# Four one-bank PSUM tiles for one four-bank tile, one store per output tile, and a new table of ranks, in a fused attention and two-layer kernel

## The chip, the cores and the metric

The kernel runs on one core of a Trainium2 chip. The metric is the device time in microseconds of one execution. Five engines work side by side: PE multiplies matrices into PSUM (eight banks of 512 floats in each of 128 partitions), DVE, ACT and POOL do elementwise work, and SP issues the transfers. Each engine takes its own instructions strictly in the order in which they were written for it, and an instruction that waits for a semaphore holds up all behind it on its engine.

## The reference, cut to what matters

Batch 2, 8 heads, 768 positions, head size 64, six hash bits; then two layers of 1536 tokens by 512 by 2048.

```
mask = q_bucket[:, :, :, None] == k_bucket[:, :, None, :]      # six sign bits of q @ proj, k @ proj
scores = np.where(mask, scale * np.matmul(q, k.transpose(0, 1, 3, 2)), -1e9)
attn = np.exp(scores - np.max(scores, axis=-1, keepdims=True))
attn = attn / (np.sum(attn, axis=-1, keepdims=True) + 1e-09)
x = np.matmul(attn, v)                       # then heads side by side: (1536, 512)
h = x @ w_in                                 # first layer
g = P(h) / (Q(h) + 1e-06)                    # cubic over quadratic in |h|
x = g @ w_out
h = x @ w_in2                                # second layer
g = h * np.clip(h + 3.0, 0.0, 6.0) / 6.0
return g @ w_out2
```

## The kernel before, in words

All values that go through PE are split into a high and a low part, and each product is three matmuls (high by high, high by low, low by high). The weights arrive as 64-bit floats in tiles of 512 KB and are converted on the chip by ACT, DVE and POOL.

**Attention** has 48 groups: 16 heads, each with three groups of 2 x 128 query rows. The names in the plan are: S, four matmuls that make the scores of 128 rows (L369 and L372) in one of two score buffers of two banks each; M, their maximum on DVE (L376); E, the exponential on ACT; A and N, the normalising; P, four transposes on PE (L403) that put a quarter of a 512-wide tile each into one bank; H, the copy of that bank to SBUF, on ACT or DVE (L413); V, the 24 matmuls with the values (L419); VO, their copies. Two groups in six do not go through P, H and V: DVE transposes them, and W (b_mm, L457) multiplies them with small 32-row tiles into all four banks, which OC and VA (b_out) then empty. TP (L244) transposes the queries and keys of a head, TF copies them out on ACT ("tf"), Z and ZB ("bt", L281 and L287) make the hash bits. SPH, SPL and SB (L268, L274, L294) are transfers on SP's queue that spread a head's parts over the operands of S; LQ and LV load queries, keys and values (L162, L172, L174).

**The layers** are 96 steps: two layers of three blocks of 512 tokens, each with 16 steps. A step has 12 matmuls into "h" (L509), the elementwise function, and 12 matmuls (L577) that add into four banks, one for each 128 outputs, over the 16 steps of a block. At the end of a block f0 and f1 empty the four banks: in layer one as a high part on ACT and a low part on DVE (L584), in layer two as a copy (L592 or ACT) that goes to the output.

**PSUM**: four of the eight banks hold the scores, and later h. The other four are handed out in turn by bank(): P, TP, Z, V and the tables at the start all take the next one. In the layers the same four are the sums of L577.

**Order**: nothing is left to a scheduler on the chip. ordered() simulates the five engines with the durations in W and picks, whenever an engine is free, the ready piece of work with the least rank; ranks are b = g * W_SLOT plus OFF and SIX. The pieces are then written in that order. Semaphore waits are put in where two instructions touch the same tile.

Of the kernel before, what the change touches and what calls it, by code (L numbers as in the profile page):

```python
# [5 lines left out]
F32 = mybir.dt.float32  # L6
# [3 lines left out]
ALU = mybir.AluOpType  # L10
# [3 lines left out]
B, H, S, D = 2, 8, 768, 64  # L14
# [12 lines left out]
NPRE = 12  # L27
NMID = 5
WARM = 8
CVS = (-4, 1, 8, 9, 11, 19, 26, 26, 36, 39, 43, 44)  # L30
RING = {"raw": 3, "cvd": 3, "t1": 2, "t2": 3, "t3": 2, "t4": 1, "gh": 2, "gl": 2}

W = {"S": 0.70, "M": 0.87, "E": 0.89, "A": 0.42, "N": 0.97, "N_A": 0.74, "B": 0.87, "W": 1.40, "P": 0.44, "H": 0.485, "H_D": 0.60, "V": 2.72, "VO": 0.35, "OC": 0.47, "VA": 0.62,
# [5 lines left out]
W_LAG = {"PE": 0.25, "DVE": 0.13, "ACT": 0.16, "POOL": 0.09, "SP": 2.5, "NONE": 0.0}  # L39
LAG = {"A": 0.30, "E": 0.26, "ld": 3.0, "LQ": 2.8}  # L40
LOOK = [0.486, 0.308]
ZERO = (0.0,) * 6
SIX = {"S": [-3.13, -2.02, -6.82, -6.23, -1.8, -1.85], "M": [24.01, 16.96, -9.66, -7.6, -7.88, -19.37], "E": [-3.33, 26.26, -14.76, 8.01, 16.22, 8.9],
# [3 lines left out]
LIKE = {("N", "ACT"): 0, ("H", "DVE"): 0.3, ("TL", "POOL"): 0, ("TH", "ACT"): 0.3, ("lo", "POOL"): 2, ("hi", "ACT"): 2}  # L47
W_SLOT = 5.7086

OFF = {"B": -4.172, "W": 17.16, "S": -18.746, "rr": -0.257, "M": 14.723, "E": -32.07, "A": 4.967, "N": -0.925, "P": 13.629, "H": 3.752, "V": -8.005,  # L50
       "VO": -33.348, "XH": 18.534, "XL": 4.581, "TP": 16.446, "Z": 11.887, "c": -5.304, "SPH": -3.253, "SPL": -22.357, "SB": -20.361, "LQ": -29.686, "LV":
       -24.74, "ld": -25.955, "cf": 5.747}
AHEAD = 0.9324
FILL = {("TP", 1, 1): 3, ("S", 1, 1): 6}
RINGS = {"T": 4, "S": 2, "p": 6, "pt": 8}

# [1 line left out]
def body(tc, q, k, v, proj, moe_w_in, moe_w_out, moe_a, moe_b, moe2_w_in, moe2_w_out, out):  # L58
    nc = tc.nc

    def act(out, in_, func=ACTF.Copy, **kw):
        nc.scalar.activation(out=out, in_=in_, func=func, **kw)  # L62
# [17 lines left out]
    atl = tc.alloc_tile_pool(name="atl", bufs=1, side="right")  # L80
    ate = tc.alloc_tile_pool(name="ate", bufs=1)
    psum = tc.alloc_tile_pool(name="psum", bufs=1, space=bass.MemoryType.PSUM)
    banks = psum.tile([128, 4, 512], F32, name="banks")
    used_banks = [0]

    def bank(n):
        used_banks[0] += 1
        return banks[:, (used_banks[0] - 1) % 4, 0:n]

    psc = tc.alloc_tile_pool(name="psc", bufs=1, space=bass.MemoryType.PSUM)  # L90

# [63 lines left out]
    nat, tf, hl, lr, live = {}, {}, {}, {}, {}  # L155
# [57 lines left out]
    for i, p in enumerate((f(pjh), pjl)):  # L213
        for isk in range(2):
            rows = slice(64 * isk, 64 * isk + 64)
            nc.vector.tensor_tensor(out=zl[rows, i, 128 + 32 * isk:128 + 32 * isk + 2 * NB].rearrange("p (a b) -> p a b", a=2),
                                    in0=p[rows].unsqueeze(1).to_broadcast([64, 2, NB]), in1=sgn[rows], op=ALU.mult)
# [135 lines left out]
    sps, ptile, pts, xts = {}, {}, {}, {}  # L353
# [91 lines left out]
    def b_mm(g, part):  # L445

        vs, pb = nat[("v", g // 3)], pts[("b", g // 3)]
        if part == 0:
            for _ in range(4):
                bank(0)  # L450
        for j in range(R * part, R * part + R):
            for i in range(4):
                rows = slice(32 * i, 32 * i + 32)
                for c in range(2):
                    x = j + NK // 2 * c
                    at = (R * (x % 4) + x // 4 - R * i) % NK
                    nc.tensor.matmul(out=banks[64 * c:64 * c + 64, i, 0:128], lhsT=vs[rows, at], rhs=pb[rows, :, 32 * x:32 * x + 32],  # L457
                                     start=(j == 0), stop=(j == NK // 2 - 1))
        if part:
            pts.pop(("b", g // 3))  # L460

    def b_out(g, part):
        main, rest = slice(64, 128), slice(0, 64)
        if part == 0:
            live["ot"] = atl.tile([128, 4, 128], F32, name="ot", tag="ot")
            act(live["ot"][main], banks[rest, :, 0:128])
            return
        nc.vector.tensor_tensor(out=xts[1][main].rearrange("p (x i k) -> p i x k", x=4, i=4),
                                in0=banks[main, :, 0:128].rearrange("p i (x k) -> p i x k", x=4),
                                in1=live["ot"][main].rearrange("p i (x k) -> p i x k", x=4), op=ALU.add)  # L470

    def x_part(g):
        hd, rg = divmod(g, 3)
# [15 lines left out]
    mps, acc = {}, {}  # L489
# [96 lines left out]
    def fin_o(m, i):  # L586
        b, r = divmod(4 * steps[m][1] + i, R)
        last = steps[m][1] == NBLK - 1
        tag = ("t3", "t2", "t1", "t3")[i] if last else "t3"
        o = mps["mp"].tile([128, 512], F32, name="o2", tag=tag, bufs=RING[tag])  # L590
        if (i % 2 == 1) != last:
            nc.vector.tensor_copy(out=o, in_=acc["o"][i])  # L592
        else:
            act(o, acc["o"][i])
        dst = out[b * S:(b + 1) * S].rearrange("(k a r) d -> r a k d", a=4, r=R)[r]
        for a in range(4):
            nc.sync.dma_start(out=dst[a], in_=o[32 * a:32 * a + 32])


    work = {}  # L600
# [7 lines left out]
    def plan_attention():  # L608
        T = W_SLOT
        pool = ("POOL",)  # L610

        def pair(pr):
# [3 lines left out]
            for hd in heads:  # L616
                if hd > 2:
                    add(("LQ", hd), ("SP", W["LQ"]), (g0 - 9 + 2 * (hd % 2)) * T + OFF["LQ"], [("TP", hd - 2, 1)], lambda e, hd=hd: load_qk(hd))
                for n in range(2):
                    r = (g0 - 9 + 2 * (hd % 2) + n) * T + OFF["TP"]  # L620

                    old = [("Z", pr - 1), ("TL", hd - 2)]
                    add(("TP", hd, n), ("PE", W["TP"]), r, [("LQ", hd)] + old, lambda e, hd=hd, n=n: tp_mm(hd, n), takes=("T",),
                        earliest=2.0 if pr == 1 else 0.0)
                    add(("TF", hd, n), ("ACT", W["TF"]), r + 0.6, [("TP", hd, n)], lambda e, hd=hd, n=n: tp_full(hd, n), frees=(("TP", hd, n),))
                add(("TH", hd), {"ACT": W["TH"], "POOL": W["TH_P"]}, r + 1.2, [("TF", hd, 0), ("TF", hd, 1), ("SPH", hd - 1), ("SPL", hd - 1)],
                    lambda e, hd=hd: tp_hi(hd, e), pool)
                add(("TL", hd), {"DVE": W["TL"], "POOL": W["TL_P"]}, r + 1.8, [("TH", hd)], lambda e, hd=hd: tp_lo(hd, e), ("POOL", "DVE"))
                r = (g0 - 4 + 3 * (hd % 2)) * T
                old = [("S", 3 * (hd - 2) + 2, 1)]  # L630
                add(("SPH", hd), ("SP", W["SPH"]), r + OFF["SPH"], [("TH", hd)] + old, lambda e, hd=hd: spread_hi(hd))
                add(("SPL", hd), ("SP", W["SPL"]), r + OFF["SPL"], [("TL", hd), ("SPH", hd)], lambda e, hd=hd: spread_lo(hd))
            r = (g0 - 5) * T + OFF["Z"]
            which = (0, 1) if pr else (1,)
# [3 lines left out]
            for hd in heads:  # L638
                r = (g0 - 4 + 3 * (hd % 2)) * T
                add(("SB", hd), ("SP", W["SB"]), r + OFF["SB"], [("ZB", pr), ("SPH", hd)], lambda e, hd=hd: spread_bits(hd))  # L640

# [4 lines left out]
        def group(g):  # L646
# [4 lines left out]
            def at(x):  # L651
                return b + OFF[x] + SIX.get(x, ZERO)[g % 6]

# [65 lines left out]
    def release_l():  # L719
        atl.release()  # L720
        wpool[2] = tc.alloc_tile_pool(name="wpool2", bufs=1, side="right", reuse_waits="tile")
        acc["o"] = [banks[:, i] for i in range(4)]

    def plan_layers():
        T = 24 * W["mm"]
        base = NG * W_SLOT
        free, due = {}, {}
# [7 lines left out]
        def add_conv(j):  # L735
            layer, u = convs[j]
            rank = base + (due[u] + 3 * NF * layer - AHEAD) * T
            if j < NPRE:
                rank = CVS[j] * W_SLOT + OFF["c"]
            key = (layer, u)  # L740
# [80 lines left out]
    def ordered():  # L821
# [28 lines left out]
        while len(out) < len(work):  # L850
# [4 lines left out]
            for when, _, n in coming:  # L855
                if n[0] in ("M", "E") and when < now + LOOK[0]:
                    soon.update((e, min(when, soon.get(e, when))) for e in work[n][0])
            while ready:
# [5 lines left out]
                if n[0] not in ("M", "E"):  # L864
                    can = [(c, e) for c, e in can if e not in soon or now + c < soon[e] + LOOK[1]]
                if can and not (kept_for.isdisjoint(takes) and room(n)):
# [3 lines left out]
                if not can:  # L870
# [3 lines left out]
                    continue  # L874
                c, e = min(can, key=lambda x: x[0] + LIKE.get((n[0], x[1]), 0.0))
                held = None if held == n else held
# [68 lines left out]
```

## Time and profile before

| | |
|---|---|
| median of three runs | 903.83 us (898.17 to 908.31) |
| the profiled execution | 902.51 us, its span 900.7 us (1.8 us lie around the span) |
| mean granted TensorE clock | 0.957 of full speed |
| PE busy | 796.1 us, 88% of the span |
| DVE, ACT, POOL busy | 558.7, 512.7, 326.9 us |

Attention fills the span up to about 350 us, the two layers the rest. A row of the chain of waits says what ended last; "idle before" of an instruction is the time that its engine stood still in front of it, with the instruction that released it.

### The profile page before, as it was taken

To read this page: it belongs to the slowest core of one execution; us is meant where nothing else is said; L and a number is where in the kernel's file an instruction comes from. 1 tells how busy PE (TensorE), PEld (TensorE's weight loads), DVE (VectorE), ACT (ScalarE), POOL (GpSimd) and SP (SyncE) were. 2 spreads that over 40 slices of the span, in tenths; PEclk is the share of its full clock that TensorE was granted. 3 is DMA by queue.
4 is the path that set the end of the run, shared out by engine and by line. 5 is a ranking of instruction groups with operands and counts; after the bars stand their busy time and mean duration, and the time that the engine had idled before them with its cause. 6 is when DMAs were issued, how large, how long until landed. Compare 5 with 4: busy or idle time off the path is not lost.

```text
span 900.7 us, 13894 instructions
## 1 busy us (share of the span) xinstructions
PE 796.1 (88%) x5179; PEld 631.8 (70%) x5179; DVE 558.7 (62%) x928; ACT 512.7 (57%) x891; POOL 326.9 (36%) x300
## 2 busy tenths in 40 slices
PE   6677776877887879999899989998999999999996
PEld 5555564665666657887688868886888788878884
DVE  3656756765565769999798879997852222222221
ACT  3765766675655778898555667887742222222221
POOL 3436456543323336677222227776740000000000
PEclk9988889898788999999999999999999999999999
DMA  7747456455644313233000012332510100010001
GB/s 173 188 136 200 129 157 173 139 144 145 170 99 122 103 36 95 71 120 115 0 1 1 9 61 70 95 117 94 187 48 0 34 14 1 1 27 20 1 1 47
DMA packets 51139, 75.29 MB, mean 84 GB/s; under 512 B 31280, under 2 KB 33024, under 8 KB 51072
## 3 DMA queue, kind: packets, MB, share of 16 engines
q1 hardware_dynamic: 50288, 74.21, 29.7%
q8 instruction: 41, 0.67, 0.3%
q10 hardware_dynamic: 784, 0.20, 0.1%
q14 instruction: 26, 0.21, 0.1%
HBM read 52.43 MB, written 3.15 MB: 62 GB/s over the span
## 4 chain that ended last, share of the span: by engine, by line
PE 75%; DVE 9%; ACT 8%; issue 2%; SPq 2%; DMA 2%; POOL 0%; DVEq 0%; ACTq 0%; POOLq 0%
PE banks L577 30%; PE h L509 27%; PE banks L403 5%; DVE pt L413 3%; PE banks L419 3%; PE banks L457 3%; ACT p L62 3%; PE s L369 2%; ACT pt L62 2%; PE s L372 2%; PE banks L244 2%; SPq L294 1%; ACT tf L62 1%; DVE xl L584 1%; ACT xh L62 1%
## 5 line engine op out<-in xcount | busy, mean ns | idle before, releaser
L137 POOL TENSOR_TENSOR cvd<-cvd,raw 128x512 int32<-128x512 int32 x64 | 89.0, 1393 | 48.3 <-DVE cvd L133 18.9
L62 ACT ACTIVATE t<-h,cbias 128x512 f32<-128x512 f32 x48 | 33.1, 689 | 125.5 <-PE h L509 125.5
L376 DVE TENSOR_REDUCE stat<-s 128x1 f32<-128x768 f32 x96 | 89.0, 948 | 20.9 <-PE s L372 20.5
L403 PE MATMUL banks<-ident,p 128*128 128x128 f32 x384 | 63.3, 309 | 43.4 <-DVE pt L413 14.9
L396 POOL TENSOR_SCALAR p<-p,stat 128x768 f32<-128x768 f32 x53 | 53.6, 1014 | 129.9 <-DVE stat L389 76.7
L566 POOL TENSOR_TENSOR gl<-t,gh 128x512 fp32r<-128x512 f32 x48 | 62.6, 1304 | 101.9 <-ACT gh L62 95.8
L65 DVE SCALAR_TENSOR_TENSOR t<-t,h 128x512 f32<-128x512 f32 x48 | 33.0, 688 | 107.2 <-ACT t L62 107.2
L62 ACT ACTIVATE p<-s,stat 128x768 f32<-128x768 f32 x96 | 85.9, 900 | 9.5 <-DVE stat L376 8.8
L62 ACT ACTIVATE gh<-t 128x512 fp32r<-128x512 f32 x96 | 60.6, 631 | 53.7 <-PE banks L577 44.4
L403 PEld LDWEIGHTS banks<-ident,p 128*128 128x128 f32 x384 | 48.0, 156 | 61.6 <-DVE pt L413 16.6
L369 PE MATMUL s<-k,q 128*128 128x384 f32 x192 | 63.4, 416 | 13.1 <-ACT p L62 13.1
L65 DVE SCALAR_TENSOR_TENSOR t<-t,coef,h 128x512 f32<-128x512 f32 x96 | 71.5, 745 | 1.8
L566 DVE TENSOR_TENSOR gl<-t,gh 128x512 fp32r<-128x512 f32 x48 | 36.5, 761 | 53.4 <-PE banks L577 48.7
L65 DVE SCALAR_TENSOR_TENSOR t<-t,r 128x512 f32<-128x512 f32 x96 | 65.9, 686 | 4.2 <-ACT r L62 1.5
L577 PE MATMUL banks<-gh,wo_0h 128*128 128x512 f32 x192 | 55.5, 396 | 8.3 <-DVE xl L584 4.3
L577 PE MATMUL banks<-wo_0h,gh 128*128 128x512 f32 x192 | 55.9, 398 | 6.5 <-DVE o L592 3.0
L413 DVE COPY pt<-banks 128x512 f32<-128x512 f32 x51 | 34.4, 689 | 41.8 <-PE banks L403 18.2
L372 PE MATMUL s<-k,q 76*128 76x384 f32 x192 | 55.9, 376 | 0.1
L577 PE MATMUL banks<-wo_0l,gh 128*128 128x512 f32 x192 | 54.9, 393 | 0.0
L577 PE MATMUL banks<-wo_0h,gl 128*128 128x512 f32 x192 | 54.9, 392 | 0.0
L577 PE MATMUL banks<-gh,wo_0l 128*128 128x512 f32 x192 | 54.8, 392 | 0.0
L577 PE MATMUL banks<-gl,wo_0h 128*128 128x512 f32 x192 | 54.8, 392 | 0.0
(149 smaller groups left out, 1924.3 us busy)
## 6 DMA issues: line engine op xcount, KB each, us to landing
raw<-in_moe_w_in_dram SPq DMA_DIRECT2D x32, 512.0 KB
raw<-in_moe_w_out_dram SPq DMA_DIRECT2D x32, 512.0 KB
q<-th SPq DMA_DIRECT2D x30, 192.0 KB
k<-th SPq DMA_DIRECT2D x30, 192.0 KB
nv<-in_v_dram SPq DMA_DIRECT2D x32, 144.0 KB
nqk<-in_q_dram SPq DMA_DIRECT2D x16, 192.0 KB
nv<-in_v_dram SPq DMA_DIRECT2D x16, 192.0 KB
nv<-in_v_dram SPq DMA_DIRECT2D x32, 96.0 KB
```

What stands on the lines that cost most here:

```text
L62: nc.scalar.activation(out=out, in_=in_, func=func, **kw)
L65: nc.vector.scalar_tensor_tensor(out=out, in0=in0, scalar=scalar, in1=in1, op0=op0, op1=op1)
L137: nc.gpsimd.tensor_tensor(out=d.bitcast(I32), in0=d.bitcast(I32), in1=raw[:, :, 0], op=ALU.add)
L369: nc.tensor.matmul(out=ps[:, n, 0:384], lhsT=q1[:, rs], rhs=k1[:, n * 384:(n + 1) * 384], start=True, stop=False)
L372: nc.tensor.matmul(out=ps[:, n, 0:384], lhsT=q2[0:KP, rs], rhs=k2[0:KP, n * 384:(n + 1) * 384], start=False, stop=True)
L376: nc.vector.tensor_reduce(out=stats[g % 4][:, rr, 0:1], in_=sps[(g, rr)][:, :, 0:384], axis=AX.XY, op=ALU.max, negate=True)
L396: nc.gpsimd.tensor_scalar(out=pt, in0=pt, scalar1=st[:, rr, 4:5], scalar2=st[:, rr, 5:6], op0=ALU.mult, op1=ALU.add)
L403: nc.tensor.transpose(ps[:, kt, rr], ptile[(g, rr)][:, (2 * i + kt) * 128:(2 * i + kt) * 128 + 128], ident)
L413: nc.vector.tensor_copy(out=pt, in_=live.pop(("p", g, i)))
L509: nc.tensor.matmul(out=ps, lhsT=w[:, ws], rhs=x[:, cols(m)], start=(n == 0), stop=(n == 3 * KD - 1))
L566: (nc.gpsimd if eng == "POOL" else nc.vector).tensor_tensor(out=e["gl"], in0=e["2"], in1=f(e["gh"]), op=ALU.subtract)
L577: nc.tensor.matmul(out=acc["o"][i], lhsT=lhsT, rhs=rhs, start=(t == 0 and n == 0), stop=(t == NF - 1 and n == 2))
```

## The change

One tile of four banks becomes four tiles of one bank. Each piece of work that read or added all four banks in one instruction (b_out) now has one instruction for each bank: four on ACT and four on DVE for one before. An output tile of 128 rows is stored by one transfer of 256 KB in place of four of 64 KB. The table of ranks, with two of the durations that the planner uses (OC and VA), is new.

```diff
-    banks = psum.tile([128, 4, 512], F32, name="banks")
+    banks = [psum.tile([128, 512], F32, name=f"bank{i}") for i in range(4)]
...
     def bank(n):
         used_banks[0] += 1
-        return banks[:, (used_banks[0] - 1) % 4, 0:n]
+        return banks[(used_banks[0] - 1) % 4][:, 0:n]
...
-                    nc.tensor.matmul(out=banks[64 * c:64 * c + 64, i, 0:128], ...
+                    nc.tensor.matmul(out=banks[i][64 * c:64 * c + 64, 0:128], ...
...
-            act(live["ot"][main], banks[rest, :, 0:128])
+            for i in range(4):
+                act(live["ot"][main, i], banks[i][rest, 0:128])
             return
-        nc.vector.tensor_tensor(out=xts[1][main].rearrange("p (x i k) -> p i x k", x=4, i=4),
-                                in0=banks[main, :, 0:128].rearrange("p i (x k) -> p i x k", x=4),
-                                in1=live["ot"][main].rearrange("p i (x k) -> p i x k", x=4), op=ALU.add)
+        for i in range(4):
+            nc.vector.tensor_tensor(out=xts[1][main].rearrange("p (x i k) -> p i x k", x=4, i=4)[:, i],
+                                    in0=banks[i][main, 0:128].rearrange("p (x k) -> p x k", x=4),
+                                    in1=live["ot"][main, i].rearrange("p (x k) -> p x k", x=4), op=ALU.add)
...
-        for a in range(4):
-            nc.sync.dma_start(out=dst[a], in_=o[32 * a:32 * a + 32])
+        nc.sync.dma_start(out=dst, in_=o)
...
-        acc["o"] = [banks[:, i] for i in range(4)]
+        acc["o"] = banks
...
-CVS = (-4, 1, 8, 9, 11, 19, 26, 26, 36, 39, 43, 44)
+CVS = (-6, 0, 9, 11, 12, 18, 30, 31, 33, 34, 34, 40)
-W_SLOT = 5.7086
+W_SLOT = 5.6039
```

What the new tables and tiles make of the order shows in three places. The first is PE, in the middle of attention: the three P tiles of one group (12 transposes; p is the normalised score tile, ident the identity). Before:

```order
L403 MATMUL banks_76<-ident_100,p_1130 128x128 [waits DVE_49,Pool_49]
L403 MATMUL banks_76<-ident_100,p_1093 128x128 [waits Pool_49]
L403 MATMUL banks_76<-ident_100,p_1130 128x128
L403 MATMUL banks_76<-ident_100,p_1093 128x128
L403 MATMUL banks_76<-ident_100,p_1130 128x128
L403 MATMUL banks_76<-ident_100,p_1093 128x128
L403 MATMUL banks_76<-ident_100,p_1130 128x128
L403 MATMUL banks_76<-ident_100,p_1093 128x128
L403 MATMUL banks_76<-ident_100,p_1130 128x128 [waits Activation_49]
L403 MATMUL banks_76<-ident_100,p_1093 128x128
L403 MATMUL banks_76<-ident_100,p_1130 128x128
L403 MATMUL banks_76<-ident_100,p_1093 128x128
```

Now, the three tiles of a group in the same part of the program:

```order
L403 MATMUL bank2_78<-ident_103,p_838 128x128 [waits Pool_49]
L403 MATMUL bank2_78<-ident_103,p_831 128x128
L403 MATMUL bank2_78<-ident_103,p_838 128x128
L403 MATMUL bank2_78<-ident_103,p_831 128x128
L403 MATMUL bank3_79<-ident_103,p_838 128x128
L403 MATMUL bank3_79<-ident_103,p_831 128x128
L403 MATMUL bank3_79<-ident_103,p_838 128x128
L403 MATMUL bank3_79<-ident_103,p_831 128x128
L403 MATMUL bank0_76<-ident_103,p_838 128x128
L403 MATMUL bank0_76<-ident_103,p_831 128x128
L403 MATMUL bank0_76<-ident_103,p_838 128x128
L403 MATMUL bank0_76<-ident_103,p_831 128x128
```

The third tile waited for an ACT copy out of another bank; here only the first instruction waits, for the normalised scores on POOL.

The second place is PE at the very end: the last step's matmuls, three for each of the four banks. Before:

```order
L577 MATMUL banks_76<-wo15_0h_1_6639,gh_7921 128x512 [waits Activation_49]
L577 MATMUL banks_76<-wo15_0l_1_6640,gh_7921 128x512
L577 MATMUL banks_76<-wo15_0h_1_6639,gl_7923 128x512 [waits DVE_49]
L577 MATMUL banks_76<-wo15_0h_1_6639,gh_7921 128x512
L577 MATMUL banks_76<-wo15_0l_1_6640,gh_7921 128x512
L577 MATMUL banks_76<-wo15_0h_1_6639,gl_7923 128x512
L577 MATMUL banks_76<-wo15_0h_1_6639,gh_7921 128x512 [waits DVE_49]
L577 MATMUL banks_76<-wo15_0l_1_6640,gh_7921 128x512
L577 MATMUL banks_76<-wo15_0h_1_6639,gl_7923 128x512
L577 MATMUL banks_76<-wo15_0h_1_6639,gh_7921 128x512 [waits Activation_49]
L577 MATMUL banks_76<-wo15_0l_1_6640,gh_7921 128x512
L577 MATMUL banks_76<-wo15_0h_1_6639,gl_7923 128x512
```

Now:

```order
L579 MATMUL bank0_76<-wo15_0h_1_6690,gh_7948 128x512 [waits Activation_49]
L579 MATMUL bank0_76<-wo15_0l_1_6691,gh_7948 128x512
L579 MATMUL bank0_76<-wo15_0h_1_6690,gl_7950 128x512 [waits DVE_49]
L579 MATMUL bank1_77<-wo15_0h_1_6690,gh_7948 128x512
L579 MATMUL bank1_77<-wo15_0l_1_6691,gh_7948 128x512
L579 MATMUL bank1_77<-wo15_0h_1_6690,gl_7950 128x512
L579 MATMUL bank2_78<-wo15_0h_1_6690,gh_7948 128x512
L579 MATMUL bank2_78<-wo15_0l_1_6691,gh_7948 128x512
L579 MATMUL bank2_78<-wo15_0h_1_6690,gl_7950 128x512
L579 MATMUL bank3_79<-wo15_0h_1_6690,gh_7948 128x512
L579 MATMUL bank3_79<-wo15_0l_1_6691,gh_7948 128x512
L579 MATMUL bank3_79<-wo15_0h_1_6690,gl_7950 128x512
```

The waits of the third and the fourth bank for the copies of the first and the second are gone; the order is the same.

The third place is SP's queue, where the operands of one head (q and k from th, tl and bt) are spread and a head's values (nv) are loaded. Before:

```order
L268 DMA q_1168<-th 64x768
L268 DMA k_1170<-th 64x768 x2
L268 DMA q_1169<-th 64x768
L274 DMA q_1168<-tl 64x768
L274 DMA k_1171<-tl 64x768
L294 DMA q_1169<-bt 12x384 x2
L294 DMA k_1171<-bt 12x384 x2
L172 DMA nv<-in_v_dram 32x1536
L172 DMA nv<-in_v_dram 32x1152
```

Now the seven value loads (the first two are shown here) and two weight loads stand ahead of the spreads from tl and bt:

```order
L268 DMA q_1213<-th 64x768
L268 DMA k_1215<-th 64x768 x2
L268 DMA q_1214<-th 64x768
L172 DMA nv<-in_v_dram 32x1536
L172 DMA nv<-in_v_dram 32x1152
...
L274 DMA q_1213<-tl 64x768
L274 DMA k_1216<-tl 64x768
L116 DMA raw<-in_moe_w_in_dram 128x1024 x2
L294 DMA q_1214<-bt 12x384 x2
L294 DMA k_1216<-bt 12x384 x2
```

The spreads from tl moved behind seven loads, those from bt behind nine.

## Rows read from the trace of the kernel before

**Rows 1.** Busy time by stage: from:to, length, busy (instructions) of each engine, PE clock, DMA.

```profile
0.00:350.00 350.00, 268.53 (x2907) 207.14 (x2908) 218.78 (x430) 224.28 (x410) 152.02 (x162) 0.89 0.53 139
350.00:901.00 551.00, 527.60 (x2273) 424.69 (x2272) 339.88 (x499) 288.40 (x482) 174.92 (x139) 1.00 0.16 48
```

**Rows 2.** Chain that ended last, 0 to 350 us, shares of that stretch.

```profile
by line: PE banks L403 13.7%; DVE pt L413 8.4%; PE banks L419 7.8%; PE banks L457 7.5%; ACT p L62 7.2%; PE s L369 5.7%; issue 5.4%; ACT pt L62 5.3%; PE s L372 4.7%; PE banks L244 3.9%; SPq L294 2.6%; ACT tf L62 2.5%; DVE stat L376 1.8%; PE
```

**Rows 3.** Who PE waited for, 0 to 350 us: total us, times, longest.

```profile
PE banks L403 <- DVE pt L413: 14.9, 17, 1.5
PE s L369 <- ACT p L62: 13.1, 9, 2.4
PE banks L403 <- ACT tf L62: 9.7, 6, 4.3
PE banks L403 <- ACT pt L62: 8.8, 11, 1.4
...
PE banks L244 <- ACT xt L62: 0.3, 1, 0.3
```

**Rows 4.** Timeline in attention: start, us, instruction, idle before and releaser.

```profile
91.45 1.04 PE L403 MATMUL banks<-ident,p 128*128 128x128 f32 x8
...
92.52 0.69 DVE L413 COPY pt<-banks 128x512 f32<-128x512 f32 x1 [0.55 <-PE banks L403]
...
93.27 0.66 PE L403 MATMUL banks<-ident,p 128*128 128x128 f32 x4 [0.79 <-DVE pt L413]
...
96.31 2.82 PE L403 MATMUL banks<-ident,p 128*128 128x128 f32 x12 [1.35 <-ACT tf L62]
```

**Rows 5.** Busy time in two stretches of 2 us in attention.

```profile
108.00:110.00 2.00, 0.11 (x1) 0.11 (x1) 2.00 (x3) 1.98 (x5) 1.09 (x2) 0.89 0.60 174
110.00:112.00 2.00, 2.00 (x8) 1.23 (x12) 1.21 (x5) 2.00 (x5) 1.92 (x2) 0.50 0.79 192
```

**Rows 6.** Who PE waited for in the layers, 350 us to the end.

```profile
PE banks L577 <- DVE xl L584: 5.8, 3, 2.2
PE banks L577 <- ACT xh L62: 3.9, 5, 1.2
PE banks L577 <- DVE o L592: 3.0, 5, 0.9
PE banks L577 <- ACT o L62: 2.1, 3, 0.7
```

**Rows 7.** Timeline at the first block's end.

```profile
437.65 0.50 PE L577 MATMUL banks<-gh,wo_0h 128*128 128x512 f32 x1 [0.69 <-ACT xh L62]
...
445.18 0.47 PE L577 MATMUL banks<-gh,wo_0h 128*128 128x512 f32 x1 [2.17 <-DVE xl L584]
```

**Rows 8.** Timeline of the end.

```profile
889.95 0.40 PE L577 MATMUL banks<-wo_0h,gl 128*128 128x512 f32 x1
...
891.10 7.38 SPq L597 DMA_DIRECT2D out_dram<-o  x16
...
891.13 0.50 PE L577 MATMUL banks<-wo_0h,gh 128*128 128x512 f32 x1 [0.78 <-DVE o L592]
...
894.58 0.60 ACT L62 ACTIVATE o<-banks 128x512 f32<-128x512 f32 x1 [1.85 <-DVE o L592]
```

**Rows 9.** Copies out of the banks by shape: busy us, mean ns of one, idle before.

```profile
L62 ACT ACTIVATE xt<-banks 64x256 f32<-64x256 f32 x18 | 6.8, 376 | 6.1 <-DVE xt L437 5.2 <-PE banks L419 0.8
L437 DVE COPY xt<-banks 64x256 f32<-64x256 f32 x14 | 5.8, 417 | 15.2 <-ACT tf L62 8.3 <-ACT xt L62 3.9 <-PE banks L244 2.9
L468 DVE TENSOR_TENSOR xt<-banks,ot 64x512 f32<-64x512 f32 x8 | 5.6, 695 | 9.2 <-ACT ot L62 9.1
...
L62 ACT ACTIVATE ot<-banks 64x512 f32<-64x512 f32 x8 | 4.7, 591 | 9.9 <-PE banks L457 9.9
```

**Rows 10.** SP's queue while one head is spread.

```profile
163.92 0.54 SPq L268 DMA_DIRECT2D q<-th  x1
...
169.23 0.47 SPq L274 DMA_DIRECT2D q<-tl  x1
```

More of the change, by code (lines that the diff above doesn't have):

```diff
@@ L29 @@
 WARM = 8
-CVS = (-4, 1, 8, 9, 11, 19, 26, 26, 36, 39, 43, 44)
+CVS = (-6, 0, 9, 11, 12, 18, 30, 31, 33, 34, 34, 40)
 RING = {"raw": 3, "cvd": 3, "t1": 2, "t2": 3, "t3": 2, "t4": 1, "gh": 2, "gl": 2}
-W = {"S": 0.70, "M": 0.87, "E": 0.89, "A": 0.42, "N": 0.97, "N_A": 0.74, "B": 0.87, "W": 1.40, "P": 0.44, "H": 0.485, "H_D": 0.60, "V": 2.72, "VO": 0.35, "OC": 0.47, "VA": 0.62,
+W = {"S": 0.70, "M": 0.87, "E": 0.89, "A": 0.42, "N": 0.97, "N_A": 0.74, "B": 0.87, "W": 1.40, "P": 0.44, "H": 0.485, "H_D": 0.60, "V": 2.72, "VO": 0.35, "OC": 1.12, "VA": 0.80,
      "XH": (0.33, 0.35, 0.60), "XL": (0.33, 0.71, 1.26), "TP": 0.33, "TF": 0.47, "TH": 0.74, "TH_P": 0.98, "TL": 0.86, "TL_P": 1.95, "Z": 0.85, "ZB": 0.59,
@@ L40 @@
 LAG = {"A": 0.30, "E": 0.26, "ld": 3.0, "LQ": 2.8}
-LOOK = [0.486, 0.308]
+LOOK = [0.735, 0.342]
 ZERO = (0.0,) * 6
-SIX = {"S": [-3.13, -2.02, -6.82, -6.23, -1.8, -1.85], "M": [24.01, 16.96, -9.66, -7.6, -7.88, -19.37], "E": [-3.33, 26.26, -14.76, 8.01, 16.22, 8.9],
[3 rows of a table removed]
-LIKE = {("N", "ACT"): 0, ("H", "DVE"): 0.3, ("TL", "POOL"): 0, ("TH", "ACT"): 0.3, ("lo", "POOL"): 2, ("hi", "ACT"): 2}
-W_SLOT = 5.7086
[L50 to L53, printed above, removed]
+SIX = {"S": [0.93, -3.97, -4.7, -7.59, 5.16, 2.43], "M": [11.03, 18.98, -5.84, -9.88, 19.32, -18.69], "E": [-25.91, 30.09, -9.92, -10.42, 66.65,
[3 rows of a table added]
+LIKE = {("N", "ACT"): 0.6, ("H", "DVE"): 1, ("TL", "POOL"): 1, ("TH", "ACT"): 2, ("lo", "POOL"): 0.3, ("hi", "ACT"): 1}
+W_SLOT = 5.6039
+OFF = {"B": -13.025, "W": 12.079, "S": -29.634, "rr": -0.101, "M": 7.649, "E": -30.203, "A": 8.548, "N": -3.697, "P": 14.532, "H": 6.109, "V": -6.154,
+       "VO": -24.39, "XH": 37.209, "XL": 5.521, "TP": 16.84, "Z": 13.301, "c": 9.562, "SPH": -21.216, "SPL": -28.51, "SB": -31.102, "LQ": -50.604, "LV":
+       -34.586, "ld": -11.253, "cf": 10.926}
+AHEAD = 4.9662
 FILL = {("TP", 1, 1): 3, ("S", 1, 1): 6}
@@ L456, in b_mm @@
                     at = (R * (x % 4) + x // 4 - R * i) % NK
-                    nc.tensor.matmul(out=banks[64 * c:64 * c + 64, i, 0:128], lhsT=vs[rows, at], rhs=pb[rows, :, 32 * x:32 * x + 32],
+                    nc.tensor.matmul(out=banks[i][64 * c:64 * c + 64, 0:128], lhsT=vs[rows, at], rhs=pb[rows, :, 32 * x:32 * x + 32],
                                      start=(j == 0), stop=(j == NK // 2 - 1))
```

6 rows, old and new, of the table SIX are left out of this document.

## Prediction

> **What bounds the kernel now.** I read first where time goes by stage, then the chain of waits in each stage, then who PE waits for, then single stretches of the timeline.
>
> By stage [rows 1] the kernel is two kernels. From 350 us on PE is busy 527.6 of 551 us: the layers are bound by PE and can lose only their small gaps. In the first 350 us no engine is full: PE has 268.5 us of work (77%), ACT 224.3 (64%), DVE 218.8 (63%), POOL 152. A stage in which three engines are each two thirds to three quarters full is bound by the way in which they wait for each other.
>
> The chain of waits in attention [rows 2] shows that way. PE's transposes L403 lead with 13.7%, and between them stand copies out of PSUM: 8.4% DVE "pt", 5.3% ACT "pt", 2.5% ACT "tf". Together 16.2% of 350 us, or 57 us, in which the end of the stage hung on a copy out of a bank and PE stood.
>
> Who PE waited for [rows 3] gives the same from PE's side. The list has 29 entries and sums to 81 us. 20 of them, from L403 behind DVE "pt" (14.9 us) down to L244 behind an ACT copy (0.3 us), are matmuls into one of the four banks behind a reader of those banks; they sum to 57.8 us. The largest other is S behind the exponential (13.1 us), the true wait for a score buffer.
>
> The timeline [rows 4] tells what kind of wait the 20 are. At 91.45 PE fills two banks with eight transposes. DVE's copy of the first starts at 92.52, after both are full: it stood 0.55 us behind a matmul that writes another bank. PE's next four go into a third bank, and yet wait 0.79 us for that copy; at 96.31 PE waits 1.35 us for ACT's copy. In the order of before, the wait stands at the third tile of a group, for a reader of a bank that this tile doesn't touch. PE's writes and the copies take turns, though four banks are there.
>
> **The change, part by part.** The sum is made against the profiled execution, 902.5 us; the median of three runs is 903.8, so the two can be read as one.
>
> *Four tiles: attention.* In the new order a matmul waits only for the reader of its own bank, and a copy only for its own bank's matmuls; the order rows of the third tile and of the last step show it, and the waits between different banks are gone on PE, ACT and DVE alike. So the 57.8 us have no cause left [rows 3]. What is late next: PE has 268.5 us of work and 81 - 57.8 = 23 us of other waits, above all S behind the exponential. Those will grow, because ACT and DVE must do the same work in a shorter time: at 300 us ACT is 75% full and DVE 73%, and each takes its queue in order. I give back 10 us, which lets the other waits grow by 40%, for engines that are 17% fuller. Attention: -48 us. [...]
>
> *Four tiles: the layers.* PE waits there 5.8 + 3.9 + 3.0 + 2.1 = 14.8 us [rows 6], all at blocks' ends: the second bank's matmuls wait 0.69 us for ACT to read the first, and the next block's first matmul waits 2.17 us for the last low part [rows 7]. By bank, the copies of one block run under the 12 matmuls of h that stand between its last sums and the next block's first, 12 matmuls or 12 x 0.232 = 2.8 us [rows 1], and a bank is needed again only after that. The first bank is then long free. I keep 1 us of it for a DVE that in these blocks is nearly full, and take out the 1.5 us that lie in the tail, counted below. Layers: -12.3 us, bounds -9 and -14.
>
> *Tail.* The last sums [rows 8]: the second bank ends at 889.95 + 0.40, then PE waits 0.78 us and 0.69 us for copies, and ACT's last copy ends at 895.18. Without the waits six matmuls follow at 527.6 / 2273 = 0.232 us [rows 1], 1.4 us, then a copy of 0.60: 892.4. The 16 transfers of the last four tiles hold SP from 891.10 for 7.38 us, 0.46 us each, till 898.5, and the span ends 2.2 us later. One transfer a tile leaves one issue behind the last copy: 892.4 + 0.46 + 2.2 = 895.1, a gain of 5.6. The last transfer carries four times the bytes, so I let it land 0.6 us later: -5, bounds -3.5 and -5.6.
>
> *Four instructions for one.* A 64x256 copy takes 376 ns on ACT and 417 on DVE, a 64x512 one 591 and 695 [rows 9]. So a column costs 0.84 and 1.09 ns, and each instruction 0.16 and 0.14 us on top. Three more of them cost 0.48 us on ACT and 0.42 on DVE, eight times: 3.9 and 3.3 us. The path from W's last matmul to xt hardly grows, since DVE adds the first bank while ACT copies the second, and both engines have a quarter of attention free; inside the 10 us given back above I count it at nothing. Uncovered it is 7 us.
>
> [...]
>
> *New ranks.* The same matmuls in a new order. The visible risk is SP: loads of values and weights now stand between the spreads of a head. In attention SP issues about 0.5 us each, and such a place exists in the trace: the spread from tl was issued 4.8 us after that from th, behind seven value loads [rows 10]. Nothing in PE's list [rows 3] is S behind a transfer, so the operands lie there in time today, and I count it at nothing. If the cover is gone it is a rival.
>
> Sum: 902.5 - 48 - 12.3 - 5 = 837.2. I forecast **837 us**.
>
> **The rivals.**
>
> *The engines give most of it back.* ACT and DVE are in-order, and a copy that no longer waits for PE meets maxima and exponentials in its own queue. For it: DVE and ACT are 100% busy in places [rows 5]. Against it: the 16.2% of the chain are copies that PE waits for, not a full engine. Attention -15, layers -11, tail -4.5: 872.
>
> [...]
>
> *SP comes last: slower.* The spreads from tl and bt now stand behind nine loads, the last two of which wait for POOL to free a buffer. Seven took 4.8 us [rows 10], so nine take 6.1. If S of each of the 14 heads from the third on has to wait that long, attention loses 86 us: 923. It decides from the point at which a head's spread is issued less than 6 us ahead of its first S. Against it: no S waits for a transfer today, and the new ranks of the spreads and of the loads of q, k and v are earlier ones.
>
> *The waits weren't on the path.* The banks are free earlier, and another wait ends at the same instant: 902. The chain [rows 2] speaks against it: it runs through the copies.
>
> **How the numbers follow.** Forecast, 820 to 855: 0.55. Better, with the clock up, about 810: 0.12. Given back, 872: 0.19. Clock down, 867: 0.07. No gain, 902: 0.03. SP, 923: 0.04. The range from 808 to 872 leaves out the last two, about half of what is given back, and some of the best cases. A change within 1%, or 9 us, can't be told from none here. Faster by over 1%: 0.92; within 1%: 0.04; slower: 0.04.
>
> **What would show it.** Right, if attention's end (the first L579 matmuls without a break) moves from about 352 to about 305 us; if PE's list no longer has L403 behind "pt" at some 15 and 9 us, but S behind the exponential leads it; if the gaps at blocks' ends vanish; and if the last store is issued within half a microsecond of the last copy. Wrong, if PE's waits for copies of the same bank, for POOL's normalising or for SP's transfers grow to tens of microseconds, or if the mean clock of attention falls below 0.85.

## The result, and the profile after

The changed kernel takes 834.31 us (median of four runs, 829.71 to 834.94) where the kernel before takes 901.0 us: a ratio of 0.925, interval 0.918 to 0.932. The profiled execution took 829.71 us (span 827.9), 72.8 us less than that of before, and 7.5 less than the 837.2 of the sum.

The first view is busy time by stage of the changed kernel, in the columns of [rows 1], here cut at the first L579 matmul and at the end of the last copy:

```profile
0.00:281.80 281.80, 244.53 (x2923) 196.17 (x2924) 217.88 (x455) 227.80 (x441) 153.36 (x169) 0.95 0.69 175
281.80:815.00 533.20, 525.70 (x2257) 425.47 (x2255) 331.76 (x492) 284.03 (x478) 170.56 (x135) 0.99 0.15 47
```

The same two stretches of before, up to the first L577 matmul and from there to the last copy:

```profile
0.00:354.00 354.00, 271.15 (x2918) 208.97 (x2919) 222.68 (x435) 228.28 (x417) 155.76 (x165) 0.89 0.53 139
354.00:895.18 541.18, 524.98 (x2263) 422.87 (x2261) 335.98 (x494) 284.40 (x475) 171.18 (x135) 1.00 0.15 47
```

Attention is 72.2 us shorter: PE stands 37.3 us in place of 82.9, and its work takes 244.5 us in place of 271.2. The layers are only 8.0 us shorter. And from the last copy to the end of the span it is 827.9 - 815.0 = 12.9 us, where before took 900.7 - 895.2 = 5.5. So the tail has become longer, not shorter.

Whom PE waited for in attention, the changed kernel's answer to [rows 3]:

```profile
PE bank L457 <- issue: 13.0, 4, 5.2
PE s L369 <- ACT p L62: 11.1, 11, 2.6
PE bank L244 <- DMA nqk<-in_k_dram: 2.6, 1, 2.6
PE bank L403 <- DVE xt L470: 2.3, 4, 0.9
PE bank L403 <- DVE pt L413: 2.3, 2, 1.5
```

The list has 10 entries with 28 waits and 36.9 us, where before had 86 waits and 82.9 us. L403 behind "pt" has gone from 14.9 + 8.8 us to 2.3. S behind the exponential, the true wait, did not grow. The new first row is a stop of L457 that waits for nothing the profile shows; its experiments are below.

The chain of waits in attention, against [rows 2]: of the copies that held 16.2% of it, only DVE's "pt" is still among the shares down to 1.8%.

```profile
by line: PE bank L403 11.4%; PE s L369 11.1%; PE bank L419 10.7%; PE s L372 8.6%; PE bank L457 7.5%; issue 7.3%; ACT p L62 4.1%; DVE stat L376 4.1%; PE bank L244 3.9%; DMA raw<-in_moe_w_in_dram 2.4%; DVE pb L443 2.1%; DVE pt L413 1.8%; DMA 
```

The timeline of the ping-pong, against [rows 4]: PE's twelve transposes into three banks run from 73.60 us without a break, while ACT, from 72.64 to 74.20, empties three banks.

```profile
72.64 1.56 ACT L62 ACTIVATE pt<-bank 128x512 f32<-128x512 f32 x3
...
73.60 1.47 PE L403 MATMUL bank<-ident,p 128*128 128x128 f32 x12
```

In the layers PE's list [rows 6] has only three entries left, and none of them lies at a block end of layer one (the third is one wait at 318 us, inside a block):

```profile
PE bank L579 <- DVE o L594: 3.4, 2, 1.7
PE bank L579 <- ACT o L62: 2.6, 2, 1.4
PE bank L579 <- ACT gh L62: 0.6, 1, 0.6
```

Where the first two come from is seen in the timeline at the end of a block of layer two:

```profile
629.73 0.60 ACT L62 ACTIVATE o<-bank 128x512 f32<-128x512 f32 x1
630.35 10.13 SPq L598 DMA_DIRECT2D out_dram<-o  x4
630.43 0.69 DVE L594 COPY o<-bank 128x512 f32<-128x512 f32 x1
636.63 0.60 ACT L62 ACTIVATE o<-bank 128x512 f32<-128x512 f32 x1 [6.30 <-DMA out_dram<-o]
...
637.28 0.50 PE L579 MATMUL bank<-wo_0h,gh 128*128 128x512 f32 x1 [1.39 <-ACT o L62]
639.22 0.69 DVE L594 COPY o<-bank 128x512 f32<-128x512 f32 x1 [8.10 <-DMA out_dram<-o]
```

The copies of the third and fourth tile find no buffer until the stores of the first and second have landed, 6.3 and 8.1 us later, and PE then waits for those copies. The chain holds 7.96 and 7.82 us of this at the two block ends of layer two; at the same place the chain of before holds 1.73 us of stores at each block end:

```profile
631.15 7.96 DMA out_dram<-o
641.62 4.65 PE h L511 x12
...
725.82 7.82 DMA out_dram<-o
```

The second row is what follows the wait: twelve matmuls of h take 4.65 us, where the chain of before has 2.72 to 2.80. Busy time in that stretch has the granted clock (third column from the end) at 0.50, where it was 1.00 from 630 to 636 us, while PE is busy all the time:

```profile
640.00:642.00 2.00, 2.00 (x5) 1.61 (x6) 1.22 (x3) 0.63 (x1) 0.00 (x0) 0.50 0.25 86
```

And the end, against [rows 8]. Between the last sums no gap is left, the stores are four issues within 3.12 us, and yet 12.9 us pass after the last copy. The second fence is busy time in such a stretch; its last two columns are the DMA share and GB/s:

```profile
813.02 3.12 SPq L598 DMA_DIRECT2D out_dram<-o  x4
...
814.41 0.60 ACT L62 ACTIVATE o<-bank 128x512 f32<-128x512 f32 x1 [0.80 <-PE bank L579]
```

```profile
820.00:822.00 2.00, 0.00 (x0) 0.00 (x0) 0.00 (x0) 0.00 (x0) 0.00 (x0) 0.50 0.26 102
```

Nothing but stores runs there, and the mean busy share of the 16 DMA engines is 0.26, at 102 GB/s. In the tail of before it was 0.51, at 133 GB/s.

### The profile page after: what moved, and what is told of

Read it like the earlier page. It is cut to its first block, busy times and chain, and to the rows that moved or that the text cites. A ratio compares the mean times of both kernels' runs of the same rounds, so it can differ in the third digit from the quotient of the medians.

```text
span 827.9 us, 13892 instructions
## 1 busy us (share of the span) xinstructions
PE 770.2 (93%) x5179; PEld 621.6 (75%) x5179; DVE 549.6 (66%) x946; ACT 511.8 (62%) x918; POOL 323.9 (39%) x303
## 4 chain that ended last, share of the span: by engine, by line
PE 75%; DVE 9%; ACT 5%; DMA 5%; issue 3%; POOL 1%; SPq 0%; DVEq 0%; ACTq 0%; POOLq 0%
PE bank L579 28%; PE h L511 28%; PE bank L403 4%; PE s L369 4%; PE bank L419 4%; PE s L372 3%; PE bank L457 3%; DVE t L65 2%; DMA out_dram<-o 2%; ACT p L62 1%; DVE stat L376 1%; PE bank L244 1%; ACT t L62 1%; DMA raw<-in_moe_w_in_dram 1%; DVE pb L443 1%
## 5 line engine op out<-in xcount | busy, mean ns | idle before, releaser
L62 ACT ACTIVATE p<-s,stat 128x768 f32<-128x768 f32 x96 | 85.8, 899 | 11.5 <-DVE stat L376 10.9
L369 PE MATMUL s<-k,q 128*128 128x384 f32 x192 | 60.5, 398 | 11.4 <-ACT p L62 11.1
L396 POOL TENSOR_SCALAR p<-p,stat 128x768 f32<-128x768 f32 x47 | 46.7, 997 | 53.1 <-DVE stat L389 40.1
L579 PE MATMUL bank<-wo_0h,gh 128*128 128x512 f32 x192 | 56.0, 398 | 6.1 <-DVE o L594 3.4
L403 PE MATMUL bank<-ident,p 128*128 128x128 f32 x384 | 54.2, 285 | 4.7 <-DVE xt L470 2.3
L403 PEld LDWEIGHTS bank<-ident,p 128*128 128x128 f32 x384 | 46.5, 147 | 12.7 <-DVE pt L413 3.2
L579 PE MATMUL bank<-gh,wo_0h 128*128 128x512 f32 x192 | 55.1, 393 | 0.7 <-ACT gh L62 0.6
L579 PE MATMUL bank<-wo_0h,gl 128*128 128x512 f32 x192 | 55.4, 395 | 0.0
L579 PE MATMUL bank<-wo_0l,gh 128*128 128x512 f32 x192 | 55.3, 395 | 0.0
L579 PE MATMUL bank<-gl,wo_0h 128*128 128x512 f32 x192 | 55.0, 393 | 0.1
L62 ACT ACTIVATE p<-p,stat 128x768 f32<-128x768 f32 x49 | 49.7, 1027 | 8.4 <-DVE stat L389 8.0
L579 PE MATMUL bank<-gh,wo_0l 128*128 128x512 f32 x192 | 54.8, 392 | 0.0
```

The lines of the kernel that those rows point to most:

```text
L369: nc.tensor.matmul(out=ps[:, n, 0:384], lhsT=q1[:, rs], rhs=k1[:, n * 384:(n + 1) * 384], start=True, stop=False)
L396: nc.gpsimd.tensor_scalar(out=pt, in0=pt, scalar1=st[:, rr, 4:5], scalar2=st[:, rr, 5:6], op0=ALU.mult, op1=ALU.add)
L403: nc.tensor.transpose(ps[:, kt, rr], ptile[(g, rr)][:, (2 * i + kt) * 128:(2 * i + kt) * 128 + 128], ident)
L579: nc.tensor.matmul(out=acc["o"][i], lhsT=lhsT, rhs=rhs, start=(t == 0 and n == 0), stop=(t == NF - 1 and n == 2))
```

## The experiments

In the first four, theory A is that the tiles bring the gain and B that the ranks do; C is that the one store costs time and D that it doesn't.

**Four tiles with the old ranks and four stores.** Against the changed kernel (the cost tables W, SIX, LIKE, OFF and the rest of the ranks' numbers as before):

```diff
-CVS = (-6, 0, 9, 11, 12, 18, 30, 31, 33, 34, 34, 40)
+CVS = (-4, 1, 8, 9, 11, 19, 26, 26, 36, 39, 43, 44)
...
-        nc.sync.dma_start(out=dst, in_=o)
+        for a in range(4):
+            nc.sync.dma_start(out=dst[a], in_=o[32 * a:32 * a + 32])
```

> The kernel before with the four one-bank tiles alone (and so with b_out in four and four instructions); old ranks, old planner durations, four stores a tile. Theory A (the waits between different banks were the cost): PE's 57.8 us of such waits in attention go, an order that was made without thought of it gives back some 10 to 25, block ends and the tail give 12 to 14: 840 to 865 us, and PE's list has no L403 behind a copy of over 5 us. Rival B (the new ranks were the gain, the tiles matter at block ends only): 885 to 895 us.

Measured: 810.68 us (807.73 to 813.63), ratio 0.899 (0.895 to 0.904). A, and more than A expected: the tiles alone are worth 90 us, and this beats the changed kernel by 24. The gain includes the clock: over whole executions the granted clock ran from 0.939 to 0.974 in the kernel before and from 0.969 to 0.979 here, and no run tells how much of that the tiles bring. Its two stretches up to the last copy:

```profile
0.00:277.10 277.10, 240.30 (x2917) 190.84 (x2918) 223.89 (x459) 226.26 (x441) 155.64 (x165) 0.94 0.70 178
277.10:798.25 521.15, 520.51 (x2263) 424.08 (x2261) 334.01 (x494) 283.40 (x475) 171.37 (x135) 1.00 0.16 48
```

From the first L579 matmul to the last copy PE stands 0.6 us in all; before it was 16.2. PE's waits at block ends are gone.

**One tile of four banks, all else as changed.**

```diff
-    banks = [psum.tile([128, 512], F32, name=f"bank{i}") for i in range(4)]
+    one_tile = psum.tile([128, 4, 512], F32, name="banks")
+    banks = [one_tile[:, i] for i in range(4)]
```

> The changed kernel with its four banks put back into one tile; new ranks, split b_out and one store a tile stay. Theory A: the waits between banks are all back, L403 behind copies some 25 to 40 us of PE, and the slow store stays: 895 to 920 us. Rival B: the ranks keep most of the gain: 845 to 865 us.

Measured: 912.78 us, ratio 1.014 (1.009 to 1.019): A. The waits of [rows 3] are back, at the new ranks:

```profile
PE banks L404 <- DVE pt L414: 15.7, 18, 1.4
...
PE banks L404 <- ACT pt L62: 10.5, 13, 1.5
```

**The changed kernel with four stores.**

```diff
-        nc.sync.dma_start(out=dst, in_=o)
+        for a in range(4):
+            nc.sync.dma_start(out=dst[a], in_=o[32 * a:32 * a + 32])
```

> The changed kernel with four stores of 64 KB a tile in place of one of 256 KB. Theory C (the one transfer is served by about 4 of the 16 DMA engines, 0.26 of them busy at 100 GB/s, so it lands late): the span ends about 7.5 us after the last copy in place of 12.9, and the waits for a free output buffer at two block ends in the second layer, 5 us each on PE, fall to 1 or 2: 818 to 825 us. Rival D (the end is late for another reason, such as the last write's receipt, whatever its shape): 828 to 835 us.

Measured: 815.72 us (814.53 to 817.94), ratio 0.905 (0.901 to 0.909): C, and 18.6 us off the changed kernel. The copies at a block end still wait for stores, but 3.2 and 4.5 us in place of 6.3 and 8.1, and PE's list no longer has a wait for these copies:

```profile
635.27 0.60 ACT L62 ACTIVATE o<-bank 128x512 f32<-128x512 f32 x1 [3.17 <-DMA out_dram<-o]
...
637.35 0.69 DVE L594 COPY o<-bank 128x512 f32<-128x512 f32 x1 [4.46 <-DMA out_dram<-o]
```

The end comes 7.7 us after the last copy. From the first L579 matmul to the end of the span it is 813.2 - 283.5 = 529.7 us, against 546.1 in the changed kernel: 16.4 us less, while attention of the profiled executions is 1.7 us longer. So the gain lies behind attention.

**The kernel before with one store.** The same line the other way round:

```diff
-        for a in range(4):
-            nc.sync.dma_start(out=dst[a], in_=o[32 * a:32 * a + 32])
+        nc.sync.dma_start(out=dst, in_=o)
```

> The kernel before with one store of 256 KB a tile, nothing else. Theory C: the end comes 12.9 us after the last copy at 895.2 in place of 5.5, and two block ends in the second layer lose 3 to 4 us more each: 910 to 918 us. Rival D: 12 issues in place of 48, 0.46 us each on SP: 896 to 902 us.

Measured: 914.25 us (906.17 to 926.22), ratio 1.018 (1.010 to 1.027): C, though the runs scatter widely. The end comes 904.4 - 893.7 = 10.7 us after the last copy, less than C's 12.9, but 5.2 more than in the kernel before, which is also what the one store costs with four tiles (12.9 against 7.7). The same rows appear in the chain:

```profile
701.90 7.45 DMA out_dram<-o
...
799.98 7.38 DMA out_dram<-o
```

**Two stores of 64 rows.** To learn why one store is slow; four tiles, old ranks:

```diff
-        for a in range(4):
-            nc.sync.dma_start(out=dst[a], in_=o[32 * a:32 * a + 32])
+        for a in range(0, 4, 2):
+            nc.sync.dma_start(out=dst[a:a + 2], in_=o[32 * a:32 * a + 64])
```

> Four tiles, old ranks, and an output tile stored in two transfers of 64 rows, 128 KB each. Theory F (the number of DMA engines that serve a transfer follows its outermost count, 4 in the one store, 32 in each of the four): the outer count is now 2, so two transfers share four engines, the DMA share after the last copy is again about 0.25, the end comes 11 to 13 us after the last copy, and layer two's block ends again wait some 8 us for a buffer: 823 to 831 us. Rival G (a transfer simply takes longer the more bytes it has, or the one store is slow because it is one): 128 KB lands in half of the 7.9 us, the end comes 7 to 9 us after the last copy and no block end waits: 809 to 814 us.

Measured: 849.32 us (847.23 to 856.29), ratio 0.945 (0.940 to 0.951). Half the bytes in a transfer made it slower still, so G falls. F has the right direction and is too mild: I let two transfers share four engines, and the trace after the last copy shows

```profile
834.00:836.00 2.00, 0.00 (x0) 0.00 (x0) 0.00 (x0) 0.00 (x0) 0.00 (x0) 0.50 0.13 51
```

that is 0.13 of 16, as much as two engines that are busy all the time, at half the rate of the one store (51 against 102 GB/s); every stretch of 2 us from 832 to 844 us has the same share. The end comes 23.4 us after the last copy, and the block ends hold 11.8 and 12.4 us of stores in the chain. So the stores with an outermost count of four kept the share at 0.26, those with one of two at 0.13, and each is the share of successive transfers together.

**Splitting b_out on one tile.** The kernel before, with its copy and its addition each in four instructions:

```diff
-            act(live["ot"][main], banks[rest, :, 0:128])
+            for i in range(4):
+                act(live["ot"][main, i], banks[i][rest, 0:128])
```

> One tile with four views as before, old ranks, four stores, and only the copy and the addition of b_out made of four instructions each. Theory (the split is covered): time as before, 897 to 906 us; with one tile and one store, split and new ranks together moved it by -1.5 us (912.8 against 914.3). Rival (the split's fixed costs, 3.9 + 3.3 us, lie open on the path): 905 to 910 us.

Measured: 901.69 us against 899.63, ratio 1.005 (1.001 to 1.009). Inside the theory's range, but not nothing: 1 to 8 us by the interval. By shape:

```profile
L471 DVE TENSOR_TENSOR xt<-banks,ot 64x128 f32<-64x128 f32 x32 | 7.3, 292 | 7.1 <-ACT ot L62 7.1
L62 ACT ACTIVATE ot<-banks 64x128 f32<-64x128 f32 x32 | 6.1, 264 | 7.0 <-PE banks L458 6.9
```

Against [rows 9] ACT is busy 1.4 us more and DVE 1.7. The mean of one is close to what the forecast's two-term price gives (0.16 us + 128 x 0.84 ns = 268 ns for ACT; 0.14 us + 128 x 1.09 ns = 280 for DVE). But the forecast added the fixed part up (3.9 and 3.3 us), and instructions that follow each other overlap: 32 x 264 ns would be 8.4 us, and ACT is busy 6.1. Four copies in a row take 0.76 us, where one for all banks took 0.59:

```profile
72.16 0.76 ACT L62 ACTIVATE ot<-banks 64x128 f32<-64x128 f32 x4 [1.33 <-PE banks L458]
...
72.95 0.92 DVE L471 TENSOR_TENSOR xt<-banks,ot 64x128 f32<-64x128 f32 x4 [1.67 <-ACT ot L62]
```

The waits in front of them fall from 9.9 to 7.0 and from 9.2 to 7.1 us; why is open. It isn't that DVE starts on the first quarter, for with one tile the four additions begin only behind the fourth copy, at 72.95 here and so in all eight places.

**Values loaded once, new ranks and old.** The 5 us between the first and the third experiment are the ranks'. This edit, on each of the two, loads v only for the first two heads, so the kernel leaves out the values of the other fourteen:

```diff
+        if hd > 1:
+            nat[("v", hd)] = nat[("v", hd % 2)]
+            return
```

> New ranks, four tiles, four stores (815.7 us), but the values of v are loaded for the first two heads only and read again by the later ones, so that 98 transfers on SP, 768 KB a head, are left out; the order of all other instructions is the same on each engine. Theory H (the 5 us that the new ranks cost are PE standing in the middle of the L457 matmuls, with no wait of their own, while its code is fetched through DMA engines that are full): these stops fall from 11.9 us to under 5, the first L579 matmul comes at 275 to 279 in place of 283.5, and the time is 806 to 812 us. Rival J (the stops or the loss belong to the order of the work): the stops stay at about 12 us, and the time is 813 to 818 us.

> Four tiles, old ranks, four stores (810.7 us), with the values of v loaded for the first two heads only, so that 98 transfers are left out. With the new ranks the same edit took 815.7 to 804.3 us, and of the 11 us only 2.7 were stops in the middle of the L457 matmuls. Theory K (what the new ranks cost is where their transfers stand, and goes with them): the old ranks gain less than the new ones did, and both meet at 801 to 806 us. Rival L (the new ranks cost it by the order of the engines' work, and the transfers cost both the same): 796 to 801 us.

Measured: 804.30 us with the new ranks (ratio 0.895, 0.890 to 0.900) and 798.52 with the old (0.887, 0.883 to 0.891). Both gain about 12 us, and 5.8 us stay between the medians: L rather than K, though the intervals touch at 0.890, and the one profiled execution with the old ranks was the slowest of its runs (803.15). The stops of PE inside L457 fall only from 11.9 to 9.2 us with the new ranks and stay (3.9 and 3.8) with the old, so most of them don't go with these transfers. That is nearer to J than to H, and 804.3 us lies in the range of neither: of the 10.9 us by which attention became shorter, 2.7 are stops, 4.3 other waits, and 3.9 PE's busy time.

What the stops are can be read from the changed kernel. This is PE's timeline at the longest one, and then busy time in three stretches within it:

```profile
149.69 2.87 PE L457 MATMUL bank<-pb,nv 32*64 32x128 f32 x162
157.77 1.15 PE L457 MATMUL bank<-pb,nv 32*64 32x128 f32 x30 [5.22 <-issue]
```

```profile
154.00:155.00 1.00, 0.00 (x0) 0.00 (x0) 0.00 (x0) 0.00 (x0) 0.83 (x3) 1.00 0.98 195
155.00:156.00 1.00, 0.00 (x0) 0.00 (x0) 0.00 (x0) 0.00 (x0) 1.00 (x1) 1.00 1.02 215
156.00:157.00 1.00, 0.00 (x0) 0.00 (x0) 0.00 (x0) 0.00 (x0) 0.10 (x1) 1.00 0.63 140
```

It stops in the middle of 192 small matmuls, 30 from their end, where no instruction has a wait; the DMA engines are full; and the DMA view of 155 to 156 us has this row, a block of program text on its way:

```profile
q8 instruction: 1, 0.02, 8.0%
```

In the three kernels with four tiles, the old ranks and all values, two stops stand 30 and 10 matmuls from the end of such a run, at the same place in each (one of the three has another, at 69). With the new ranks there are four of them, of 1.4 to 5.2 us in the changed kernel. The traces' packets tell more. All eleven profiled executions together have 30 such stops, of 0.3 to 5.2 us, and every one ends 1.2 to 1.7 us after a block of 16 KB on this queue has landed: here the block lands at 156.4 us and PE goes on at 157.8. So a stop ends with the arrival of code, which makes code the likely thing that PE waits for. Why these blocks come late, and whether full DMA engines delay them, no experiment isolated.

**The last stores on two queues.** Four tiles, old ranks, four stores, and of the last sixteen the last six issued by ACT:

```diff
+            if last and 4 * i + a >= 10:
+                ends.append((dst[a], o[32 * a:32 * a + 32]))
...
+        if last and i == 3:
+            for d, src in ends:
+                nc.scalar.dma_start(out=d, in_=src)
```

> Four tiles, old ranks, four stores (810.7 us), and of the last 16 stores the last six are issued by ACT's queue behind its last copy. Theory (after the last copy the end is SP's row of issues, 0.46 us each, of which 5.4 us lie behind the copy): SP's ten are out after 4.6 us, ACT's six after 2.8, both about 2.7 us earlier than before, and the end comes 5 us after the last copy in place of 7.7: 807 to 809 us. Rival (the transfers themselves are the end, or ACT's issues are dearer): 810 to 812 us.

Measured: 809.44 us (807.83 to 810.54), ratio 0.899 (0.896 to 0.903). The trace does what the theory said: SP's ten and ACT's six issues end within 0.8 us of each other, and the end comes 807.7 - 802.4 = 5.3 us after the last copy in place of 7.7. The 2.4 us can't be told from the first experiment's 810.68 in the runs; no kernel that keeps the whole computation was faster than these two.

```profile
800.43 4.99 SPq L604 DMA_DIRECT2D out_dram<-o  x10
801.81 0.60 ACT L62 ACTIVATE o<-bank 128x512 f32<-128x512 f32 x1 [0.80 <-PE bank L579]
801.87 2.78 ACTq L607 DMA_DIRECT2D out_dram<-o  x6
```

## Why the prediction came out right, and which of its steps did not

The time lay 3 us from the forecast by the median, and that nearness is luck: two terms were off by much in opposite directions. By the profiled executions: attention -72.2 where the sum has -48; from there to the last copy -8.0 where it has -15.1 (12.3 for block ends and 2.8 of the tail term); after the last copy +7.4 where it has -2.2. The differences are -24.2, +7.1 and +9.6, together the 7.5 us between 837.2 and 829.7.

**Attention: right in its mechanism, too small in size.** The banks' waits went, as the second experiment shows by bringing them back. PE's standing time fell by 45.6 us, and the term has 48. The 10 us given back in it came true by size and not by reason: S behind the exponential was to grow and went from 13.1 to 11.1 us, while the stops inside L457, which the term didn't have, grew from 2.9 to 13.0. What was missing is PE's busy time, -26.6 us; the forecast left less work on PE to the case of 810 us, 27 below it, with a chance of 0.12. The runs part it in two. The kernel before with one store has the same attention as before, but its profiled execution had a granted clock of 0.95 there:

```profile
0.00:339.60 339.60, 254.46 (x2917) 193.97 (x2918) 223.00 (x435) 227.57 (x417) 155.50 (x165) 0.95 0.56 145
```

So some 17 us (271.2 to 254.5) go with the clock, and in attention that varied between executions of one-tile kernels (0.89, 0.95, 0.93, 0.93) more than of four-tile kernels (0.92 to 0.95). At the same 0.95 the change still takes PE's work from 254.5 to 244.5 us and its standing time from 85.1 to 37.3. An estimate for those 10 us of work: an out matmul (L577) lasts 389 ns (the median up to 420 us in the trace of before) and the next starts 232 ns after it [rows 1], so a stop behind one leaves 0.16 us of it uncovered; 58 stops fewer would make 9 us. That is only worked out, from matmuls of the layers while most stops stood at transposes, and it wasn't tried alone.

Two cases, 867 us with the clock down and 810 with it up, rest on estimates of mine alone, 30 us above the forecast and 27 below, and no run shows these terms. What the runs show in their place: the clock of attention was 0.89 in the profiled execution of before and 0.95 in the changed kernel's, and with one tile the step from 0.89 to 0.95 took some 17 us off PE's busy time.

**Layers: right in its mechanism, too small in size.** With four stores the stretch to the last copy goes from 541.2 to 522.0 us (third experiment) and 521.2 (first), -19 to -20 against -15.1; PE's idle time there went from 16.2 to 1.5 and 0.6 us, and in the third experiment its busy time from 525.0 to 520.5. The changed kernel gives 11.2 us of this back, by the next step and not by the banks: PE stands 6.0 us more, and it is busy 5.2 us more, since behind the wait it goes on at a clock of 0.50, as the row of 640 us shows.

**Tail and store: wrong, in sign.** The step that failed is "the last transfer carries four times the bytes, so I let it land 0.6 us later". I counted SP's issues, which did fall, and took the transfer's own time as given. At a block end it landed some 8 us after its issue (7.96 and 7.82 us in the chain), and where nothing but such stores runs the DMA share is 0.26, as much as four of the 16 engines that are busy all the time, for all the stores under way together (256 KB at the measured 102 GB/s are 2.6 us for each, an estimate). That costs 5.2 us after the last copy against four stores (12.9 against 7.7) and 11.2 at two block ends, where I hadn't looked at all: the next copies need the two buffers whose stores are under way. Removing it gained 18.6 us, adding it to before cost 13.6 by the medians (9 to 24 by the interval). The shares go with the outermost counts of the stores: 0.26 with 4 groups of 32 rows in one transfer, 0.13 with 2 groups in each of two transfers, and 0.51 and 0.54 in the tails of before and of the third experiment, with four transfers of 32 rows. Why a count goes with a share was not shown, and which engines they are, no view here tells. The measurement decides for four stores of 32 rows, 815.72 us against 834.31.

**The split of b_out: nearly right.** Counted at nothing, it costs something between 1 and 8 us alone, median 2. Uncovered it was to be 7 us, and ACT and DVE are busy only 1.4 and 1.7 us more. The cover that I gave for it, DVE adding the first bank while ACT copies the second, doesn't show in the changed kernel, where the additions begin at least 1 us behind the last copy.

**New ranks: not nothing, but 5 us.** No S waits for a spread as in the rival at 923 us. With four tiles and four stores attention ends at 283.5 us in place of 277.1. The stops of PE inside L457 are 11.9 against 3.9 us there, a wait that stood in before's list only with 2.9 us and that I hadn't read. But other waits are shorter, so that PE stands only 1.5 us more; its busy time is 4.9 us more, at a clock of 0.92 against 0.94, of which six matmuls of the layers that now stand earlier are 6 x 0.232 = 1.4 us. Which of these the ranks cost is open.

**What the views were to show.** L403 behind "pt" vanished and the gaps at layer one's block ends did, as written. The gaps at layer two's first two block ends stayed, 6.0 us in all, now for the sake of the stores. S behind the exponential is second, not first. Attention's end came at 282, not 305. The last store was issued within half a microsecond of the last copy, as written, and the span still ended later: that sign was chosen badly, since it says nothing of the landing.

## What to carry to other kernels

Four banks in one tile with four views make reader and writer of different banks wait for each other; of 57.8 us of such waits PE's standing time lost 46 to 48 here, and 10 us of busy time went with them at the same clock. Before several stores are joined into one, look at the DMA share in a stretch with nothing else running: here it was 0.26 with an outermost count of four, 0.13 with one of two and 0.51 to 0.54 with four stores of 32 rows. And it was the landing of a store, not its issue, that freed the buffer behind it: the copies waited 6.3 and 8.1 us for it. A wait can cost more than its length: behind the stop at 640 us the clock was 0.50, and twelve matmuls of h took 4.65 us in place of 2.72 to 2.80. A forecast that comes out right by sum should still be checked stage by stage: here the change as made hides a loss of 24 us behind a gain of 90.

## What was not expected of the hardware

Two transfers of 128 KB a tile, issued one after the other, kept the share of the 16 DMA engines at 0.13 together, half the 0.26 of one of 256 KB, and the end came later (23.4 against 12.9 us after the last copy). And PE stopped up to 5.2 us in the middle of a run of small matmuls that wait for nothing, and each of 30 such stops ended 1.2 to 1.7 us after a block of instructions had landed.
